# Talking-heads attention with a squared-ReLU feed-forward: queries loaded and turned in two parts, loads moved, four squares on VectorE, values products and transposes in front of score bursts

## The chip, the cores and the metric

One Trainium2 chip; the kernel runs on one of its cores. The metric is device time in microseconds (us) of one execution. The engines are named as in the profile: PE is TensorE (matmuls; PEld its weight loads), DVE VectorE, ACT ScalarE, POOL GpSimd, SP SyncE. PSUM has eight banks, which matmuls write and ACT and DVE read; SBUF is the working memory.

## What is computed

```
B, H, S, D = 8, 12, 448, 64
scores = (q @ k^T) / 8                               # per batch and head
scores = einsum('bhij,hg->bgij', scores, w_pre)      # heads mixed
attn   = softmax(scores over j)
attn   = einsum('bhij,hg->bgij', attn, w_post)       # heads mixed again
x      = (attn @ v), as [8*448, 768]
out    = (max(x @ w_in, 0) ** 2) @ w_out             # 768 -> 2048 -> 768
```

Inputs and output are f32 in HBM; on the chip operands are bf16 and sums f32.

## The kernel before

**Steps.** The attention of a batch is cut into 45 steps of up to ten queries (`IQ`), 360 steps in all. In a step the 120 rows of one tile are 10 queries x 12 heads, so that a matmul with a 120x120 matrix mixes the heads. `mix` (L456) does the first mix, one matmul into `m_ps` (L467), and the exponential on ACT (L471), with its sums; DVE takes the reciprocal `rc` (L478); POOL scales the second mixing matrix to `pn` (L481) and, for the last 64 keys, `en` (L484). `unmix` (L487) comes `LAG` = 4 steps later: three or four matmuls into `at_ps` (L496, L500) that mix and turn at once, and a copy to `at` on DVE (L502). Fifteen steps make a third of a batch, and `av_unit` (L246) then multiplies it with the values into `ot_ps` (L254, L261; two units a third) and copies it on ACT to `xt` (L267).

**Scores.** `score_burst` (L394) computes six heads of a block of up to 128 queries (L406; the last block of a batch packs its 64 queries in L412), each head into a PSUM bank, and ACT and DVE copy them to a tile `S`, of which there are two. `gather` (L423) copies ten queries' rows of all heads from `S` to a tile `G` by a DMA on SP's queue, ten steps (`AHEAD`) before the step that reads it; there are twelve `G`. `BURSTS` says at which gathered step of a block the two bursts of the next block are issued.

**Batch 0's first twenty steps** have no `S`: DVE multiplies the turned queries with the mixing weights (`mix_queries`, L218, into `w`, `tails` and `xt`), and `fused_part` (L445) takes six matmuls a step straight from keys and weighted queries into `m_ps` (L453). Steps 0 to 3 are weighted first (`NEAR`), then to 12 (`SOON`), then to 20 (`FUSED`).

**Queries, keys, values, weights.** POOL's queue loads them with a cast to bf16. Batch 0's queries and keys come in twelve loads, two of six heads a time, queries and keys in turn (L109 to L114); later batches in four loads (`load_qk`, `KQ_AT`, `KQ_LATER`: the steps), values in three (`load_v`, `V1_AT`, `V_LATER`), the FFN's weights in six and eight (`W1_AT`, `W2_AT`). Each query and key tile has one buffer, so a load waits until the batch before is turned. `turn_unit` (L227) does that: 28 transposes of 64x64 a unit and operand pair (L239) into two banks, and two copies (L241); six units a batch, at the steps of `TURN`.

**FFN.** `ffn1_unit` (L301): matmuls into `h_ps` (L308), ReLU on ACT to `hr` (L314), squares on POOL (L320; on DVE for the last third of batch 0). `ffn2_unit` (L347): eight matmuls a half (L353), the sum copied on DVE (L362) and stored.

**Order.** The order of PE and POOL is the program's own (`manual_schedule`); DVE, ACT and SP are ordered by a planner when the kernel is built, but for `issue_after`, which puts instructions behind a given one. Within a step: `mix`, then the units set for the step (`at_step`, `timed`: turns, value products), a share of the FFN's units (`fill`), `unmix`, up to two gathers with a burst where one is due, and another share. After a burst a second half of `ffn2_unit` is taken ahead, since it needs no new bank. A value product is set three steps after its third's last `unmix`; in the same step as the third third's product, the batch's FFN units join the list. `still` (L93) issues matmuls on zeros, whose result is not used, between the first transposes (`STILL`).

Of the kernel before, what the change touches and what calls it, by code (L numbers as in the profile page):

```python
# [14 lines left out]
B, H, S, D = 8, 12, 448, 64  # L15
DMODEL = H * D
DFF = 2048
NPAIR = H // 2
FT = DFF // 128
R = 4  # L20
RQ = 7
PQ = S // RQ
HQ = H // 2
IQ = 10
NT = 45
RG = H * IQ
FUSED = 20
# [5 lines left out]
BURSTS = {0: ([4, 8], [5, 8])}  # L33
for _b in range(1, B):
    STARTS[_b], FIRST[_b], BURSTS[_b] = (0, 128, 256, 384), (0, 13, 26, 39), ([5, 8], [5, 8], [6], [2, 4])
BURSTS[1] = ([5, 8], [7, 10], [6], [2, 4])
BURSTS[2] = ([7, 10], [5, 8], [6], [2, 4])
GATHERS_AT = 8
FIRST_AT = (3, 5, 7)
HALF = H // 2  # L40
TT = 15
TQ = TT * IQ
LAG = 4
AHEAD = 10
SCALE = 1.0 / 8.0
TURN = {0: (20, 22, 23, 24, 26, 27), 1: (24, 24, 24, 28, 28, 28), B: (2 + LAG,) * 3 + (17 + LAG,) * 3}
KQ_LATER = {1: (26, 28, 37, 41), B: (22, 25, 28, 31)}
V_LATER = {1: (30, 32, 34), B: (34, 37, 40)}
KQ_AT = {1: (4, 7, 10, 12), 2: (49, 51, 53, 55)}
W1_AT = (-1, 1, 3, 14, 16, 18)  # L50
W2_AT = (27, 29, 31, 33, 36, 39, 42, 45)
V1_AT = (46, 48, 24)
EARLY = ((21, 0, 0, 2), (29, 0, 2, 4), (38, 1, 0, 4), (52, 2, 0, 4))
FFN2_AT = 60
STILL = (10, 2, 2, 2, 1)
SOONEST = 3
MAIN = 3 * 128


@with_exitstack  # L60
def kernel(
# [36 lines left out]
    def stage_tile(name):  # L98
        return stage.tile([P, HQ, RQ, D], BF16, name=name, tag=name, bufs=1)

    def load(t, src, b, a, h0=0, h1=HQ):

        nc.gpsimd.dma_start(out=t[PQ * a:PQ * a + PQ, h0:h1, :, :].rearrange("p h r d -> p h (r d)"),
                            in_=src[b, HQ * a + h0:HQ * a + h1, :, :].rearrange("h (p r) d -> p h (r d)", r=RQ))

    staged = {}
    staged[0] = (stage_tile("qst"), stage_tile("kst"))
    ident = consts.tile([P, P], BF16, name="ident")
    for u in range(NPAIR // 2):  # L109
# [108 lines left out]
    def mix_queries(u, t0, t1):  # L218

        for y in range(2):  # L220
            qs = qTs[0][:, u + 3 * y, IQ * t0:IQ * t1].rearrange("p (t i) -> p t i", i=IQ)
            mixes[(u, t0)] = nc.vector.tensor_tensor(out=mixed(u, y, t0, t1).rearrange("p (t g i) -> p t g i", g=H, i=IQ),
                                    in0=qs.unsqueeze(2).to_broadcast([P, t1 - t0, H, IQ]),
                                    in1=wrep[:, u + 3 * y, :, :].unsqueeze(1).to_broadcast([P, t1 - t0, H, IQ]),
                                    op=ALU.mult)

    def turn_unit(b, which, u, eng=None):  # L227

        store, name = (qTs, "qT") if which == 0 else (kTs, "kT")
        if b not in store:  # L230
            store[b] = work.tile([P, NPAIR, S], BF16, name=name, tag=name, bufs=2)
        src = staged[b][which]
        got = [bank("tr_ps", BF16) for _ in range(2)]
        for r in range(RQ):
            c = PQ * (r if which == 0 or r == RQ - 1 else 2 * (r % 3) + r // 3)
            for hh in range(2):
                for x in range(2):
                    rs = slice(PQ * x, PQ * x + PQ)
                    nc.tensor.transpose(got[x][64 * hh:64 * hh + 64, c:c + PQ], src[rs, 2 * u + hh, r, :], ident[rs, rs])  # L239
# [61 lines left out]
    def ffn1_unit(b, ft, k=1, n0=0, n1=S):  # L301

        ps = bank("h_ps")
        n = n1 - n0
        for j in range(k):
            f = ft + j
            for c2 in range(NPAIR):
                nc.tensor.matmul(ps[:, n * j:n * j + n], lhsT=w1[f // 8][:, c2, f % 8 * 128:f % 8 * 128 + 128],  # L308
                                 rhs=xts[b][:, c2, n0:n1], start=(c2 == 0), stop=(c2 == NPAIR - 1))
        if n0 == 0 and ft % 2 == 0:  # L310
            h2ts[(b, ft // 2)] = ffnp.tile([P, 2, MAIN], BF16, name="h2", tag="h2", bufs=FT // 2 + 1)
        h2 = h2ts[(b, ft // 2)][:, ft % 2:ft % 2 + k, :]
# [211 lines left out]
    with tc.manual_schedule(engines={PE, POOL}):  # L524
# [19 lines left out]
        with tc.issue_after(mixes[(2, 0)].ins):  # L544
            mix_queries(1, NEAR, SOON)
            mix_queries(2, NEAR, SOON)
        loads = {}
        ahead = [FUSED]

# [26 lines left out]
        bounds = sorted({x[0] for x in EARLY} | {FFN2_AT, 2 * NT + 1 + LAG})  # L576
        end = len(steps) + LAG + 3
        for i in range(-1, end):
            for f in loads.get(i, []):
# [15 lines left out]
            rest = early[0] - i if early else (1 + LAG - i) % NT + 1  # L595
# [19 lines left out]
            if 2 < i < 6:  # L615
                with tc.issue_after(mixes[(2, NEAR)].ins):
                    mix_queries(i - 3, SOON, FUSED)
            if i in FIRST_AT:
                x = 2 * FIRST_AT.index(i)
                score_burst(0, 0, [x, x + 1])  # L620
            if i == 3:
                with tc.issue_after(mixes[(2, NEAR)].ins):
                    make_post()
                    make_orders()
                    clear_values()
            for _ in range(2 if i >= GATHERS_AT else 0):
                if ahead[0] > min(max(i + AHEAD, FIRST[0][1] - 1), len(steps) - 1):
                    break
                b2, t2 = steps[ahead[0]]
                gather((b2, t2))  # L630
                ahead[0] += 1
                blk2 = max(x for x in range(len(FIRST[b2])) if FIRST[b2][x] <= t2)
                nxt = blocks.index((b2, blk2)) + 1
                first = BURSTS[b2][blk2]
                if nxt < len(blocks) and t2 - FIRST[b2][blk2] in first:
                    x = first.index(t2 - FIRST[b2][blk2])
                    score_burst(*blocks[nxt], [3 * x, 3 * x + 1, 3 * x + 2])
                    if filler and filler[0][1] in second:
                        w, f = filler.pop(0)
                        f()  # L640
                        owed[0] -= w
            if i + 1 < end:
                fill(share)
        for j in sorted(timed):
# [34 lines left out]
```

## Time and profile before

| | us |
|---|---|
| Median of 3 runs | 583.04 (582.56 to 585.91) |
| The profiled execution | 583.95 |
| Its span in the profile | 582.2 |
| PE busy | 567.5 (97%) |
| DVE busy | 398.8 (69%) |
| ACT busy | 379.7 (65%) |
| POOL busy | 378.9 (65%) |
| First exponential of step 0 starts at | 16.43 |
| Step 0 of batch 1, 2, 3 and 4 (start of its exponential) | 73.6, 133.2, 201.3, 266.3 |

The span runs from the first to the last instruction; the execution's own time has 1.75 us around it. A line of a group gives the engine, the operation, names of what is written and read, the shape, the count, busy time and mean duration. In a timeline, the first number is the start, the second the time from there to the end of the group, and the bracket the idle time of the engine before it and what ended it. Matmuls overlap in the pipe, so a duration of 0.2 to 0.35 us is a latency; the distance between two starts is what a matmul costs.

### The profile page before, as it was taken

How to read it: one execution, taken by the hardware profiler on the slowest of the kernel's cores; microseconds unless marked ns; L12 is line 12 of the kernel's file. 1: busy time of each engine (PE TensorE's matmuls, PEld its weight loads, DVE VectorE, ACT ScalarE, POOL GpSimd, SP SyncE). 2: the span in 40 equal slices, each digit the busy share in tenths (PEclk: the TensorE clock that was granted, in tenths of full speed). 3: DMA queues.
4: the chain of work that ended last, by engine and by line, in shares of the span. 5: the costliest groups of instructions: out<-in, count | busy, mean ns of one | idle time of the engine just before them, and what ended most of it. 6: DMA issues, size and time to landing. Idle time of an engine off the chain costs nothing.

```text
span 582.2 us, 18463 instructions
## 1 busy us (share of the span) xinstructions
PE 567.5 (97%) x6750; PEld 362.6 (62%) x6752; DVE 398.8 (69%) x980; ACT 379.7 (65%) x1090; POOL 378.9 (65%) x844
## 2 busy tenths in 40 slices
PE   7999999999999999999999999999999999999996
PEld 3667777556566566566566665666665665666554
DVE  6858868778676777866877668867877668655011
ACT  2768978588876557864877648775777548862410
POOL 6657985655877448774778547785577647774830
PEclk9999999999999999999999999999999999999999
DMA  9999998797568864796558954697544865422113
GB/s 130 159 193 184 187 199 173 152 168 175 111 108 149 145 128 87 126 157 141 101 100 135 176 117 93 120 145 154 107 73 71 137 139 104 84 46 55 29 27 82
DMA packets 84043, 72.28 MB, mean 124 GB/s; under 512 B 18768, under 2 KB 80496, under 8 KB 83952
## 3 DMA queue, kind: packets, MB, share of 16 engines
q0 software_dynamic: 37856, 33.04, 37.1%
q1 hardware_dynamic: 45514, 37.86, 29.5%
q8 instruction: 53, 0.87, 0.6%
q10 hardware_dynamic: 582, 0.21, 0.2%
q14 instruction: 38, 0.31, 0.1%
HBM read 47.28 MB, written 11.01 MB: 100 GB/s over the span
## 4 chain that ended last, share of the span: by engine, by line
PE 89%; DMA 6%; ACT 2%; POOL 1%; issue 1%; DVE 1%; ACTq 0%; POOLq 0%
PE h_ps L308 24%; PE o_ps L353 24%; PE m_ps L467 11%; PE at_ps L496 10%; PE ot_ps L254 5%; DMA G<-S 5%; PE s_ps L406 5%; PE m_ps L453 4%; PE tr_ps L239 2%; PE ot_ps L261 2%; PE at_ps L500 2%; DMA kst<-in_k_dram 1%; PE s_ps L412 1%; ACT e L471 1%; ACT S L416 1%
## 5 line engine op out<-in xcount | busy, mean ns | idle before, releaser
L502 DVE CAST at<-at_ps 128x480 bf16<-128x480 f32 (+1 forms) x360 | 206.6, 592 | 63.1 <-PE at_ps L500 46.0
L471 ACT ACTIVATE e<-m_ps 120x448 bf16<-120x448 f32 x360 | 195.7, 550 | 82.1 <-PE m_ps L467 45.4
L481 POOL TENSOR_SCALAR pn<-post,rc 120x120 bf16<-120x120 bf16 (+1 forms) x340 | 122.4, 370 | 137.6 <-DVE rc L478 76.0
L308 PE MATMUL h_ps<-xt,w 128*128 128x448 bf16 (+2 forms) x960 | 165.8, 315 | 1.0 <-ACT S L416 0.9
L353 PE MATMUL o_ps<-w,h 128*128 128x384 bf16 x768 | 138.8, 326 | 0.1
L467 PE MATMUL m_ps<-G,pre 120*120 120x448 bf16 (+1 forms) x340 | 121.3, 357 | 2.5 <-ACT S L416 1.4
L308 PEld LDWEIGHTS <-w 128*128 128x128 bf16 x960 | 83.4, 98 | 54.1 <-issue 4.9
L496 PE MATMUL at_ps<-pn,e 120*128 120x120 bf16 x1080 | 115.8, 215 | 1.3 <-POOL pn L481 1.1
L496 PEld LDWEIGHTS <-e 120*128 120x128 bf16 x1080 | 85.9, 98 | 45.7 <-issue 3.6
L320 POOL TENSOR_TENSOR h<-hr 128x384 bf16<-128x384 f32 (+1 forms) x128 | 103.1, 806 | 11.1 <-ACT hr L314 9.5
L353 PEld LDWEIGHTS <-h 128*128 128x128 bf16 x768 | 72.4, 98 | 50.5 <-issue 8.0
L314 ACT ACTIVATE hr<-h_ps 128x448 f32<-128x448 f32 (+2 forms) x136 | 72.0, 530 | 47.0 <-PE h_ps L308 39.4
L416 ACT CAST S<-s_ps 128x448 bf16<-128x448 f32 x177 | 82.3, 551 | 11.1 <-PE s_ps L406 7.2
L418 DVE CAST S<-s_ps 128x448 bf16<-128x448 f32 x141 | 80.0, 615 | 3.9 <-DMA G<-S 2.8
L471 ACT ACTIVATION_READ_ACCUMULATOR e<-m_ps 120x1 f32 x360 | 75.5, 210 | 0.0
L362 DVE COPY osb<-o_ps 128x384 f32<-128x384 f32 x54 | 30.0, 556 | 55.4 <-PE o_ps L353 55.3
L478 DVE RECIPROCAL rc<-sm 120x1 f32<-120x1 f32 (+1 forms) x192 | 31.0, 162 | 40.6 <-ACT e L471 28.0
L467 PEld LDWEIGHTS <-pre 120*120 120x120 bf16 (+1 forms) x340 | 45.0, 132 | 17.5 <-issue 8.6
L267 ACT CAST xt<-ot_ps 128x450 bf16<-128x450 f32 (+1 forms) x48 | 25.7, 534 | 26.7 <-PE ot_ps L261 26.3
L484 POOL TENSOR_TENSOR en<-e,rc 120x128 bf16<-120x128 bf16 (+1 forms) x112 | 42.8, 382 | 0.0
L254 PE MATMUL ot_ps<-at,v 128*64 128x150 bf16 x864 | 41.7, 229 | 0.0
L406 PE MATMUL s_ps<-kT,qT 64*128 64x448 bf16 x276 | 39.0, 352 | 0.2
(66 smaller groups left out, 502.7 us busy)
## 6 DMA issues: line engine op xcount, KB each, us to landing
G<-S SPq DMA_DIRECT2D x276, 105.0 KB
out_dram<-osb POOLq DMA_DIRECT2D x48, 192.0 KB, 4.7
kst<-in_k_dram POOLq DMA_DIRECT2D x14, 336.0 KB, 5.9
qst<-in_q_dram POOLq DMA_DIRECT2D x14, 336.0 KB, 5.8
G<-S SPq DMA_DIRECT2D x70, 52.5 KB
v<-in_v_dram POOLq DMA_DIRECT2D x8, 384.0 KB, 9.1
w<-in_moe_w_in_dram POOLq DMA_DIRECT2D x6, 512.0 KB, 8.5
w<-in_moe_w_out_dram POOLq DMA_DIRECT2D x8, 384.0 KB, 9.2
```

The costliest lines, as they stand in the source:

```text
L254: nc.tensor.matmul(ps[64 * hh:64 * hh + 64, TQ * y:TQ * y + TQ], lhsT=vts[b % 2][:, g, r, :], rhs=at[:, r, g, :, :].rearrange("p t i -> p ...
L308: nc.tensor.matmul(ps[:, n * j:n * j + n], lhsT=w1[f // 8][:, c2, f % 8 * 128:f % 8 * 128 + 128], rhs=xts[b][:, c2, n0:n1], start=(c2 == 0 ...
L314: nc.scalar.activation(out=hr[:, 0:k * n], in_=ps[:, 0:k * n], func=ACT.Relu)
L320: eng.tensor_tensor(out=dst[:, :, x - o:y - o], in0=hr[:, :, x - n0:y - n0], in1=hr[:, :, x - n0:y - n0], op=ALU.mult)
L353: nc.tensor.matmul(ps[:, 0:384], lhsT=lhsT, rhs=w2[ft // 4][:, ft % 4, nt * 384:(nt + 1) * 384], start=(ft == 0), stop=(ft == FT - 1))
L416: nc.scalar.copy(out=sb[:, h, :], in_=ps[:, 0:S])
L418: nc.vector.tensor_copy(out=sb[:, h, :], in_=ps[:, 0:S])
L467: nc.tensor.matmul(ps[0:n, 0:S], lhsT=m[0:n, 0:n], rhs=Gs.pop(s)[0:n, :], start=True, stop=True)
L471: nc.scalar.activation(out=e[0:n, x, :], in_=ps[0:n, 0:S], func=ACT.Exp, scale=SCALE, accum_out=sm[0:n, x:x + 1])
L481: nc.gpsimd.tensor_scalar(out=esb[(b, t - z)][1][0:rows, :], in0=(post_gi if fused else post)[0:rows, :], scalar1=rc[0:rows, z:z + 1], sca ...
L496: nc.tensor.matmul(ps[:, RG * r:RG * r + RG], lhsT=e[0:n, tl % 2, P * r:P * r + P], rhs=pn[0:n, :], start=True, stop=True)
L502: nc.vector.tensor_copy(out=ats[(b, third)][:, 0:k, :, tl, :], in_=ps[:, 0:k * RG].rearrange("p (r g i) -> p r g i", r=k, i=IQ))
```

## The change

- *Queries in two parts.* Batch 0's queries are loaded as two of their seven row groups (`RF` = 2, 128 of 448 queries) for all heads first, in two loads with rows of 256 bytes in bf16; then the keys in six loads; then the other five row groups in two loads. The identity's memset is on DVE, and its mask comes after the fourth key load. `turn_unit` takes a range of row groups: the first part is turned at the start, the rest at step 3 (`REST_AT`). Weighted queries come in pieces of four steps, and one copy of the last keys is on DVE.
- The first score bursts of batch 0, the first gather and the last weighted queries come one step later.
- *Loads spread:* batch 2's queries and keys at steps 52, 54, 58, 61, batch 3's keys at 22 and 24 of batch 1, batch 2's values at 53, 55, 57 of batch 1, one load of batch 1's values at 49. The last two bursts in batch 1 come one step later.
- *Four squares:* of batch 0's second third, the squares of the FFN's upper half are on DVE.
- *Directly in front of bursts:* from batch 1 on, a third's value products are set in the step of the next burst that is three to seven steps away, directly in front of it (else as before); from batch 2 on, so are the transposes, at steps 8 (keys) and 22 (queries), which were at 6 and 21. Batch 0's transposes come in pairs, batch 1's first three at 20 instead of 24.
- `still`: 13, 3 and 3 matmuls instead of 10, 2, 2, 2 and 1.

```diff
@@ constants @@
+RF = 2
...
-BURSTS[1] = ([5, 8], [7, 10], [6], [2, 4])
+BURSTS[1] = ([5, 8], [7, 10], [6], [3, 5])
 BURSTS[2] = ([7, 10], [5, 8], [6], [2, 4])
-GATHERS_AT = 8
-FIRST_AT = (3, 5, 7)
+GATHERS_AT = 9
+FIRST_AT = (4, 6, 8)
+REST_AT = 3
...
-TURN = {0: (20, 22, 23, 24, 26, 27), 1: (24, 24, 24, 28, 28, 28), B: (2 + LAG,) * 3 + (17 + LAG,) * 3}
-KQ_LATER = {1: (26, 28, 37, 41), B: (22, 25, 28, 31)}
-V_LATER = {1: (30, 32, 34), B: (34, 37, 40)}
-KQ_AT = {1: (4, 7, 10, 12), 2: (49, 51, 53, 55)}
+TURN = {0: (21, 21, 24, 24, 27, 27), 1: (20, 20, 20, 28, 28, 28), B: (8,) * 3 + (22,) * 3}
+KQ_LATER = {1: (22, 24, 37, 41), B: (22, 25, 28, 31)}
+V_LATER = {1: (53, 55, 57), B: (34, 37, 40)}
+KQ_AT = {1: (4, 7, 10, 12), 2: (52, 54, 58, 61)}
...
-V1_AT = (46, 48, 24)
+V1_AT = (46, 49, 24)
...
-STILL = (10, 2, 2, 2, 1)
+STILL = (13, 3, 3)
+MERGE = 8
@@ first loads @@
-    def load(t, src, b, a, h0=0, h1=HQ):
-        nc.gpsimd.dma_start(out=t[PQ * a:PQ * a + PQ, h0:h1, :, :].rearrange("p h r d -> p h (r d)"),
-                            in_=src[b, HQ * a + h0:HQ * a + h1, :, :].rearrange("h (p r) d -> p h (r d)", r=RQ))
+    def load(t, src, b, a, h0=0, h1=HQ, r0=0, r1=RQ):
+        nc.gpsimd.dma_start(out=t[PQ * a:PQ * a + PQ, h0:h1, r0:r1, :].rearrange("p h r d -> p h (r d)"),
+                            in_=src[b, HQ * a + h0:HQ * a + h1, :, :].rearrange("h (p r) d -> p h (r d)", r=RQ)[:, :, r0 * D:r1 * D])
...
+    for x in range(2):
+        load(staged[0][0], q, 0, x, r1=RF)
+    nc.vector.memset(ident[:, :], 0.0)
     for u in range(NPAIR // 2):
-        for w, src in enumerate((q, k)):
-            for x in range(2):
-                load(staged[0][w], src, 0, x, 2 * u, 2 * u + 2)
-                if u + w == 0 and x == 1:
-                    masks.make_identity(nc, ident[:, :])
+        for x in range(2):
+            load(staged[0][1], k, 0, x, 2 * u, 2 * u + 2)
+        if u == 1:
+            masks.make_identity(nc, ident[:, :], nomemset=True)
+    for x in range(2):
+        load(staged[0][0], q, 0, x, r0=RF)
@@ turn_unit @@
-    def turn_unit(b, which, u, eng=None):
+    def turn_unit(b, which, u, engs=None, r0=0, r1=RQ):
...
-        for r in range(RQ):
+        for r in range(r0, r1):
...
-            (eng or nc.vector.tensor_copy)(out=store[b][:, u + 3 * x, :], in_=got[x][:, 0:S])
+            copy = engs[x] if engs else nc.vector.tensor_copy
+            copy(out=store[b][:, u + 3 * x, PQ * r0:PQ * r1], in_=got[x][:, PQ * r0:PQ * r1])
@@ ffn1_unit @@
-        eng = nc.vector if n0 >= 2 * TQ else nc.gpsimd
+        eng = nc.vector if n0 >= 2 * TQ or n0 and ft >= FT // 2 else nc.gpsimd
@@ order of the start @@
-    timed = {}
+    timed, front = {}, {}
+    burst_at = sorted(NT * b + FIRST[b][x] + y - AHEAD for b in range(1, B) for x in range(4) for y in BURSTS[b][x]
+                      if (b, x) != (B - 1, 3))
...
         for u in range(NPAIR // 2):
-            turn_unit(0, 0, u)
+            turn_unit(0, 0, u, r1=RF)
             mix_queries(u, 0, NEAR)
-            if u == 1:
-                with tc.issue_after(mixes[(1, 0)].ins):
-                    mix_queries(0, NEAR, SOON)
+        still(STILL[1])
+        for u in range(NPAIR // 2):
             if u == 2:
+                with tc.issue_after(mixes[(2, 0)].ins):
+                    mix_queries(0, NEAR, 2 * NEAR)
+
+            def between(out, in_):
+                with tc.issue_after(mixes[(0, NEAR)].ins):
+                    mixes["kT"] = nc.vector.tensor_copy(out=out, in_=in_)
+
+            turn_unit(0, 1, u, (nc.scalar.copy, nc.scalar.copy if u < 2 else between))
+            if u == 0:
+                still(STILL[2])
+            else:
                 for t in range(SOONEST):
-                    fused_part(t, 0)
-            else:
-                still(STILL[1 + 2 * u])
-            turn_unit(0, 1, u, nc.scalar.copy)
-            if u < 2:
-                still(STILL[2 + 2 * u])
-        for t in range(SOONEST):
-            fused_part(t, 1)
...
+        for t0 in range(NEAR, SOON, NEAR):
+            with tc.issue_after(mixes["kT" if t0 == NEAR else (2, t0 - NEAR)].ins):
+                for u in range(t0 == NEAR, NPAIR // 2):
+                    mix_queries(u, t0, t0 + NEAR)
@@ order of the steps @@
                         for x, u in enumerate(turn_units(b + 1)):
-                            at_step(i + TURN.get(b, TURN[B])[x], u)
+                            if b in TURN:
+                                at_step(i + TURN[b][x], u)
+                            else:
+                                front.setdefault(i + TURN[B][x], []).append(u)
...
                 if t1 % TT == TT - 1:
+                    j = min([x for x in burst_at if 3 <= x - i < 8 and b1] + [i + MERGE])
                     for u in av_units(b1, t1 // TT):
-                        at_step(i + 3, u)
-                if t1 == NT - 1:
-                    at_step(i + 3 if b1 else FFN2_AT, (0, lambda b1=b1: filler.extend(ffn_units(b1))))
...
+                        if j in burst_at and b1:
+                            front.setdefault(j, []).append(u)
+                        else:
+                            at_step(i + 3, u)
+                    if t1 == NT - 1:
+                        more = (0, lambda b1=b1: filler.extend(ffn_units(b1)))
+                        if not b1:
+                            at_step(FFN2_AT, more)
+                        elif j in burst_at:
+                            front.setdefault(j, []).append(more)
+                        else:
+                            at_step(i + 3, more)
+            if i == REST_AT:
+                for u in range(NPAIR // 2):
+                    turn_unit(0, 0, u, r0=RF)
...
                     x = first.index(t2 - FIRST[b2][blk2])
+                    for w, f in front.pop(i, []):
+                        f()
+                        owed[0] -= w if not FFN2_AT <= i < 2 * NT else 0
                     score_burst(*blocks[nxt], [3 * x, 3 * x + 1, 3 * x + 2])
```

The bounds by which the FFN's units are spread over a batch's steps end two steps later (`3 + LAG` for `1 + LAG`), as the units start two steps later.

More of the change, by code (lines that the diff above doesn't have):

```diff
@@ L528 @@
         for u in range(NPAIR // 2):
-            turn_unit(0, 0, u)
+            turn_unit(0, 0, u, r1=RF)
             mix_queries(u, 0, NEAR)
-            if u == 1:
-                with tc.issue_after(mixes[(1, 0)].ins):
-                    mix_queries(0, NEAR, SOON)
+        still(STILL[1])
+        for u in range(NPAIR // 2):
             if u == 2:
-                for t in range(SOONEST):
-                    fused_part(t, 0)
-            else:
-                still(STILL[1 + 2 * u])
-            turn_unit(0, 1, u, nc.scalar.copy)
-            if u < 2:
-                still(STILL[2 + 2 * u])
-        for t in range(SOONEST):
-            fused_part(t, 1)
-        with tc.issue_after(mixes[(2, 0)].ins):
-            mix_queries(1, NEAR, SOON)
-            mix_queries(2, NEAR, SOON)
+                with tc.issue_after(mixes[(2, 0)].ins):
[7 more added lines that the diff above has]
+            else:
+                for t in range(SOONEST):
+                    fused_part(t, u - 1)
+        for t0 in range(NEAR, SOON, NEAR):
+            with tc.issue_after(mixes["kT" if t0 == NEAR else (2, t0 - NEAR)].ins):
+                for u in range(t0 == NEAR, NPAIR // 2):
+                    mix_queries(u, t0, t0 + NEAR)
         loads = {}
@@ L575 @@
             at_step(x, (0, lambda third=third, q0=q0, q1=q1: begin(ffn1_third(third, q0, q1))))
-        bounds = sorted({x[0] for x in EARLY} | {FFN2_AT, 2 * NT + 1 + LAG})
+        bounds = sorted({x[0] for x in EARLY} | {FFN2_AT, 2 * NT + 3 + LAG})
         end = len(steps) + LAG + 3
@@ L592 @@
                         for x, u in enumerate(turn_units(b + 1)):
-                            at_step(i + TURN.get(b, TURN[B])[x], u)
+                            if b in TURN:
+                                at_step(i + TURN[b][x], u)
+                            else:
+                                front.setdefault(i + TURN[B][x], []).append(u)
             early = [x for x in bounds if x > i]
-            rest = early[0] - i if early else (1 + LAG - i) % NT + 1
+            rest = early[0] - i if early else (3 + LAG - i) % NT + 1
             rest = min(rest, end - i) if i > len(steps) - NT // 2 else rest
@@ L610 @@
                 if t1 % TT == TT - 1:
+                    j = min([x for x in burst_at if 3 <= x - i < 8 and b1] + [i + MERGE])
                     for u in av_units(b1, t1 // TT):
-                        at_step(i + 3, u)
-                if t1 == NT - 1:
-                    at_step(i + 3 if b1 else FFN2_AT, (0, lambda b1=b1: filler.extend(ffn_units(b1))))
-            if 2 < i < 6:
-                with tc.issue_after(mixes[(2, NEAR)].ins):
-                    mix_queries(i - 3, SOON, FUSED)
+                        if j in burst_at and b1:
[13 more added lines that the diff above has]
+                    turn_unit(0, 0, u, r0=RF)
+            if FIRST_AT[0] <= i < FIRST_AT[0] + 3:
+                with tc.issue_after(mixes[(2, SOON - NEAR)].ins):
+                    mix_queries(i - FIRST_AT[0], SOON, FUSED)
             if i in FIRST_AT:
@@ L621 @@
             if i == 3:
-                with tc.issue_after(mixes[(2, NEAR)].ins):
+                with tc.issue_after(mixes[(2, SOON - NEAR)].ins):
                     make_post()
@@ L641 @@
                         owed[0] -= w
+            for w, f in front.pop(i, []):
+                f()
+                owed[0] -= w
             if i + 1 < end:
```

## The prediction

> **What bounds the kernel now.** I read the page's busy table, then stretches of the span, the waits of the one bad stretch, and timelines where work of the change stands.
>
> ```profile
> PE 567.5 (97%) x6750; PEld 362.6 (62%) x6752; DVE 398.8 (69%) x980; ACT 379.7 (65%) x1090; POOL 378.9 (65%) x844
> ```
>
> TensorE is the bound: the others have a third of the span free. A gain must come from TensorE's idle time or from its lost time between matmuls. The busy time by stretches says where it idles (columns: stretch, its length, then busy time and instructions of PE, PEld, DVE, ACT, POOL; clock, DMA share, GB/s):
>
> ```profile
> 60.00:100.00 40.00, 37.57 (x529) 29.36 (x526) 31.02 (x83) 34.23 (x107) 31.81 (x69) 1.00 1.04 190
> 100.00:140.00 40.00, 37.63 (x625) 24.53 (x624) 30.31 (x76) 28.60 (x86) 23.38 (x59) 1.00 0.85 165
> ...
> 200.00:300.00 100.00, 99.80 (x1311) 63.37 (x1310) 75.31 (x185) 68.98 (x200) 68.98 (x156) 1.00 0.63 118
> ```
>
> From 60 to 140 us, the end of batch 0 and all of batch 1, TensorE idles 2.43 + 2.37 = 4.8 us; from 200 to 300 only 0.2. The waits from 55 to 150 us (total, times, longest) name what it waited for:
>
> ```profile
> ACT S L416 <- DMA G<-S: 3.1, 2, 2.6
> ...
> PE m_ps L467 <- ACT S L416: 1.4, 1, 1.4
> ...
> PE at_ps L496 <- POOL pn L481: 1.1, 1, 1.1
> ```
>
> The 1.4 is a wait for score copies that still hold the PSUM banks, and they waited themselves until gathers had read the old S; the 1.1 is a late `pn` on POOL. A third, 0.87 before `h_ps` at 88.57, is again a wait for score copies. At the start, the chain runs through the last key load:
>
> ```profile
> 14.33 0.41 PE L239 MATMUL tr_ps<-ident,kst 64*64 64x64 bf16 x27 [0.61 <-DMA kst<-in_k_dram]
> ...
> 14.67 3.62 PE L453 MATMUL m_ps<-kT,w 128*120 128x448 bf16 x18
> ...
> 16.43 0.54 ACT L471 ACTIVATE e<-m_ps 120x448 bf16<-120x448 f32 x1 [0.68 <-PE m_ps L453]
> ```
>
> From 14.67 on TensorE never waits long, so what lets it begin earlier is worth its full time. Last, what a change of the matmuls' form costs in the steady state:
>
> ```profile
> 318.85 0.35 PE L467 MATMUL m_ps<-G,pre 120*120 120x448 bf16 x1
> 319.04 0.32 PE L496 MATMUL at_ps<-pn,e 120*128 120x120 bf16 x3
> 319.20 0.35 PE L467 MATMUL m_ps<-G,pre 120*120 120x448 bf16 x1
> 319.48 0.39 PE L254 MATMUL ot_ps<-at,v 128*64 128x150 bf16 x6
> ...
> 320.76 0.25 PE L261 MATMUL ot_ps<-at,v 128*64 128x80 bf16 x4
> 320.84 0.38 PE L254 MATMUL ot_ps<-at,v 128*64 128x150 bf16 x6
> 321.03 0.25 PE L261 MATMUL ot_ps<-at,v 128*64 128x80 bf16 x4
> 321.22 0.33 PE L496 MATMUL at_ps<-pn,e 120*128 120x120 bf16 x3
> ```
>
> After `m_ps`, `at_ps` starts 0.19 us later but `ot_ps` 0.28: going to the half-width form costs 0.09. After the last `ot_ps` group the next start is 0.19 us away instead of 0.08: leaving costs 0.11.
>
> **The start: loads.** Before, twelve loads of 112 KB; issues on POOL about 0.59 us apart; the last key load is issued at 8.41 and lands at 14.29 (the trace's DMA records); the five before it land 4.6 us after their issue (4.14 and less for the first ones), the last 5.9. After, two query loads of 384 runs each (0.69 us on POOL, as the later whole loads of 384 runs at 27.04 and 31.82; the first 0.2 more), then six key loads at 0.60 and the mask step of 0.35 between (its memset goes to VectorE): the last key load is issued at 1.28 + 0.89 + 0.69 + 4 x 0.60 + 0.35 + 0.60 = 6.2. By 4.6 it lands at 10.8, 3.5 us earlier; by 5.9 at 12.1, 2.2 earlier. By packets: 896-byte packets took 88 ns, 384-byte 51, 128-byte 32, so 256-byte ones some 41 (an estimate on that line), and 896-byte packets passed at 216 per us, 19 in flight. Query part 768 x 41 / 19000 = 1.7 us, keys 768 / 216 = 3.6, against 1536 / 216 = 7.1 before: 1.8 us earlier. Ends 1.8 and 3.5; I take 3.2, since the 4.6 held for five loads out of six.
> The first packet rows show no break, only a slope. The Trainium skill's "DMA: Bandwidth & Descriptors" (Specifications) says that below 512 bytes a DMA does a read-modify-write and loses line rate; the query part writes 256 bytes per run. By the slope it is 1.7 us; if that rule doubled it (the page has no factor; an estimate), the start would gain 1.7 us less and the sum come to 577.0. No row here has 256 bytes.
>
> **The start: work moved.** The other five sevenths of the queries are turned at step 3, no longer under a load wait but in TensorE's full stream: 60 of 84 transposes; 84 take 0.93 us at 296.39, so 0.66, plus 0.09 and 0.11 for the forms: 0.86. Their loads are the next two in POOL's queue (v and w1 one place later, not needed before step 21). They are wanted at about 14.5 and land at 13.8 to 15; I take no wait, at most 1.0. VectorE's mixes up to step 12 total the same, in more pieces; it has all first queries at 7 instead of 11.85 us, which covers six more issues and one key copy (0.35). If this cover is gone the exponentials wait 1 us. Extra still matmuls (19 for 17) lie under the load wait. Net 3.2 - 0.9 = 2.3; ends 1.8 - 0.9 - 1.0 = -0.1 and 2.8.
>
> **Stalls of 60 to 140 us.** Before the stall at 78.80, POOL did squares at 76.27 and 77.72 (0.70 each) and a value load (0.80, at 76.90) ahead of the `pn`. The two squares go to VectorE: `pn` 1.4 us earlier, and the 1.09 is gone; I take 1.0. The squares, 300 wide, cost VectorE 0.46 us each by its rows of 128 and 168 elements (0.28 and 0.33), up to 0.9 when it runs beside POOL's (0.50 and 0.77 at 84.7); VectorE is 78% busy there, and they may wait on ACT's `hr` (0.55 the longest). Queued behind them are `at` copies and `rc`, so `pn`; each has four steps in hand, about 6 us. Price without that cover 4 x 0.55 = 2.2.
> At 117.52, score copies waited 2.64 us for gathers and TensorE lost 1.42, so 1.2 were covered. Batch 1's last bursts come one step later (about 1.5 us), leaving 1.1, which is covered; the value and key loads around it move to other steps (their issues stay 0.7 to 0.8 each on POOL). I take 1.3. At 88.57 (0.87) and the small ones (0.30, 0.33): the next batch's loads are spread from steps 49-55 to 52-61, so the gathers have fewer packets beside them; 0.7 together. SP issues the gathers in order; after batch 1's last burst its first gather from that S comes one step later, with ten steps in hand. Sum 3.0; ends 4.8 (all gone) and -1 (they move and VectorE's squares bring one).
>
> **Merged visits.** Values products with transposes, directly before a burst, save one visit to the narrow forms: 0.09 + 0.11 less a direct change of form. That change's price: from the last transpose to the first value product 0.12 us at ten places, so 0.10 net. By the burst steps, 18 merges: 2 in batch 1, 3 in each of 2 to 6, 1 in 7: 1.8 us. Ends 0 and 3.6. Batch 0's six turns are in three pairs: 3 x 0.2 = 0.6. Together 2.4. Nothing else is removed: matmuls, copies and exponentials are the same. The moved units' copies move with them (ACT 2 x 0.53, VectorE 6 x 0.31), and FFN units start and end two steps later.
>
> **Sum.** 2.3 + 3.0 + 2.4 = 7.7 us. The profiled execution took 583.95 (span 582.2 and 1.75 around it), 0.91 above the median of 583.04: it would become 576.25, the median 575.3.
>
> **Rivals.**
> *Banks run out in front of the bursts* (the slower side). At steps 8 and 22 of batches 2 to 6 fourteen banks' worth is written in a row, with eight to be had. TensorE needs 0.93 + 1.7 + 0.8 = 3.4 us for it; VectorE six copies in 1.87 and three of 0.616, 3.7, and its `at` copies. If each of the ten places loses what 117.52 lost (1.42, the next bank) and what the burst at 164.54 lost (0.58, its own banks), that is 20.0, and the median 595.3. It decides from 0.77 us a place (7.7 / 10); over 1% slower from 1.35. Against it: at 296.39 transposes and value products end at 299.06 and the 12-matmul burst at 299.72 starts 0.25 us after the matmul before it; nearly the same pile, no wait.
> *The start gains nothing*: VectorE or the second query part is late. 583.04 - 5.4 = 577.6.
> *The stalls move*: S has two buffers before and after, and the gathers must read the old one. 583.04 - 4.7 = 578.3.
> *All ends good*: 2.8 + 4.8 + 4.2 = 11.8, so 571.2.
> *TensorE's clock falls while it waits for keys.* The first 512-column matmuls here came 0.43 us apart, the 18 of 448 columns at 14.67 0.20. At the early pace (0.376 for 448) the 24 of steps 0 to 3 cost 4.2 more: 579.5. Against it: the waits before were as long (0.96), the rows give a granted clock of 1.00 throughout, and the faster pace held. The Trainium skill's "TensorE: Matmul & The Clock Gate" (What's actually happening) has half rate after an idle window of about 3.4 us; the trace's first matmuls agree, and none of the new waits should be that long.
>
> **How the numbers follow.** Forecast 0.56, with its own range 571.5 to 578.5; all good 0.10; start lost 0.07; stalls move 0.08; clock 0.03; banks 0.16. About 1% (5.8 us, 577.2 and 588.9) is what a measurement can tell. Faster by over 1%: all good, 0.10, and of the forecast 0.46, together 0.56. Within 1%: the forecast's other 0.10, the start lost, the stalls and the clock, together 0.28. Slower by over 1%: banks, 0.16. Range 567 to 586: it holds every case but most of the banks' (586 is 1.1 a place), and below 567 lies only more than all good.
>
> **What would show it.** Right: the first `e` at 13 to 13.5 us instead of 16.43; 60 transposes in the stream behind step 3 without a DMA wait; TensorE busy over 38.5 of 40 us in the two stretches; no `pn` wait near 77; `ot_ps` with the next start an `s_ps`. Wrong: `s_ps` or `tr_ps` waiting for `S` or `qT` copies in batches 2 to 6; VectorE's `w` as the last releaser of `m_ps`; a slow first 12 us.

## The result, and the profile after

| | before | after |
|---|---|---|
| median, us (18 runs each) | 583.08 (581.25 to 586.71) | 585.92 (583.86 to 588.35) |
| ratio after / before | | 1.0051 [1.0032, 1.0069] |
| the profiled execution, us | 583.95 | 583.95 |
| its span, us | 582.2 | 581.6 |
| first exponential of step 0 starts at, us | 16.43 | 12.8 |

The change costs half a per cent, where 1.3% less was forecast. The profiled execution of the changed kernel lies 2 us under its median, so its trace shows less than the whole loss; two more traces of it are used below. Part of the loss lies outside the span: the changed kernel's runs have 2.25 to 2.36 us around it, where before's have 1.8 on average.

The busy table of the changed kernel, and the same stretches as in the prediction with one more (length, then busy time and instructions of PE, PEld, DVE, ACT, POOL; clock, DMA share, GB/s):

```profile
PE 568.2 (98%) x6753; PEld 363.9 (63%) x6754; DVE 405.0 (70%) x998; ACT 377.6 (65%) x1089; POOL 376.9 (65%) x837
```

```profile
60.00:100.00 40.00, 38.96 (x645) 30.56 (x642) 34.30 (x92) 34.08 (x105) 29.17 (x64) 1.00 1.04 196
100.00:140.00 40.00, 38.40 (x557) 24.61 (x558) 32.36 (x81) 30.89 (x95) 23.55 (x59) 1.00 0.73 152
200.00:300.00 100.00, 99.44 (x1300) 62.90 (x1298) 76.05 (x188) 69.54 (x202) 67.11 (x150) 1.00 0.65 119
300.00:400.00 100.00, 98.72 (x1084) 61.30 (x1083) 76.36 (x171) 67.03 (x194) 68.82 (x155) 1.00 0.73 131
```

The two bad stretches got better, as forecast: TensorE idles 1.04 + 1.60 us instead of 4.8. The steady state got worse: 0.56 us idle from 200 to 300 instead of 0.20, and 1.28 instead of 0.17 in the next hundred. What TensorE waits for is new as well (total, times, longest):

```profile
PE s_ps L420 <- issue: 1.6, 1, 1.6
PE s_ps L414 <- ACT e L479: 1.4, 8, 0.2
...
PE s_ps L414 <- DVE at L510: 0.8, 2, 0.4
```

The first row is a single wait in the packed burst of batch 2; "issue" means that the profile shows nothing that it waited for, so its cause stays open. In the other rows score matmuls wait until ScalarE's exponential has read an `m_ps`, or VectorE's copy an `at_ps`: for a free bank. Before has one such wait, of 0.6 us.

The rows hold only the last piece of each wait; matmuls that start late one after another count as busy in the pipe. To see it all I took the starts of all matmuls between 20 and 540 us and subtracted what each needs when it streams. Inside the score bursts 9.7 us are lost that way, against 2.7 in before's trace; in two more traces of after 9.9 and 9.2, and 2.1 in a second one of before. Some 1.9 of the 9.7 are the unexplained wait in batch 2 (0.9 and 1.4 in the two other traces); the rest is the loss that the experiments below follow up. Where it falls is seen at step 8 of batch 4, in TensorE's timeline of the changed kernel (start, time to the group's end, ...):

```profile
271.92 1.05 PE L246 MATMUL tr_ps<-ident,kst 64*64 64x64 bf16 x84
272.90 0.39 PE L262 MATMUL ot_ps<-at,v 128*64 128x150 bf16 x6
...
274.64 1.07 PE L414 MATMUL s_ps<-kT,qT 64*128 64x448 bf16 x6
...
276.88 1.16 PE L414 MATMUL s_ps<-kT,qT 64*128 64x448 bf16 x5
...
278.22 0.35 PE L414 MATMUL s_ps<-kT,qT 64*128 64x448 bf16 x1 [0.18 <-ACT e L479]
...
278.50 1.31 PE L316 MATMUL h_ps<-xt,w 128*128 128x448 bf16 x6
```

Transposes, value products and the first burst stand together as the change wants it, and that burst takes 1.00 us to the next start. The *next* burst follows 2.24 us after it, and its six matmuls take 1.62 us, 276.88 to 278.50. From 271.9 to 278.50 no FFN matmul is issued. In before's trace, at the same step, FFN matmuls (`h_ps`) stand between the two bursts, which are 4.47 us apart, and the second takes 0.69 us (282.89 to 283.58):

```profile
278.42 0.85 PE L406 MATMUL s_ps<-kT,qT 64*128 64x448 bf16 x6
...
279.77 1.30 PE L308 MATMUL h_ps<-xt,w 128*128 128x448 bf16 x6
...
281.30 1.30 PE L308 MATMUL h_ps<-xt,w 128*128 128x448 bf16 x6
...
282.89 0.74 PE L406 MATMUL s_ps<-kT,qT 64*128 64x448 bf16 x6
283.58 0.38 PE L467 MATMUL m_ps<-G,pre 120*120 120x448 bf16 x1
```

The busy times of VectorE (the third) and ScalarE (the fourth) in the changed kernel say why the banks are not back:

```profile
271.90:278.50 6.60, 6.42 (x172) 4.15 (x170) 6.46 (x19) 4.89 (x15) 2.21 (x5) 1.00 0.50 109
274.70:278.50 3.80, 3.62 (x28) 1.56 (x26) 3.80 (x11) 3.75 (x12) 0.45 (x2) 1.00 0.53 127
```

From 274.7 on both engines that empty the banks are busy almost without a break, 3.80 and 3.75 of 3.80 us. VectorE copies the six turned keys, half of twelve score banks and every `at`; ScalarE copies the value products and the other half of the score banks, and has the exponentials behind them. The releases in the trace show both: the second burst's matmuls start after a score copy and an `at` copy on VectorE and after three exponentials on ScalarE, and the last two, 0.30 and 0.53 us after the one before, after exponentials. So it is not VectorE alone.

The burst after step 8's loses in each of batches 2 to 6: 0.94 in batch 2 and 1.05 in the others (0.11 to 0.40 before, where the two are 3.4 to 4.5 us apart). The merged burst of step 8 itself loses 0.25 in batch 2 and 0.44 in the others (0.22 before). Other bursts lose in some batches only: 0.88 and 0.85 at step 31 of batches 4 and 5, and 1.30 at step 43 of batch 5 (393.59).

Why no FFN matmuls? The FFN is spread over the steps by an account. Every unit set in front of a burst is charged to it, `owed[0] -= w`: three turn units of 250 and two value products of 800, so 2350 at once, which stops the FFN's units for about three steps. Before, the same 2350 were charged at step 6, where these transposes and products stood together (from 274.75 in its trace), two steps ahead of the burst of step 8, so that FFN units came again before the burst after it.

### The profile page after: what moved, and what is told of

It reads as the page before. It is cut to its first block, busy times and chain, and to the rows that moved or that the text cites. A ratio compares the mean times of both kernels' runs of the same rounds, so it can differ in the third digit from the quotient of the medians.

```text
span 581.6 us, 18472 instructions
## 1 busy us (share of the span) xinstructions
PE 568.2 (98%) x6753; PEld 363.9 (63%) x6754; DVE 405.0 (70%) x998; ACT 377.6 (65%) x1089; POOL 376.9 (65%) x837
## 4 chain that ended last, share of the span: by engine, by line
PE 85%; DMA 5%; ACT 5%; DVE 2%; POOL 1%; issue 1%; SPq 0%; ACTq 0%; POOLq 0%
PE o_ps L361 25%; PE h_ps L316 24%; PE m_ps L475 11%; PE at_ps L504 9%; PE ot_ps L262 5%; PE s_ps L414 4%; DMA G<-S 4%; ACT e L479 3%; PE m_ps L461 2%; PE tr_ps L246 2%; PE ot_ps L269 2%; PE at_ps L508 2%; ACT S L424 1%; PE s_ps L420 1%; DMA kst<-in_k_dram 1%
## 5 line engine op out<-in xcount | busy, mean ns | idle before, releaser
L504 PEld LDWEIGHTS <-e 120*128 120x128 bf16 x1080 | 88.3, 98 | 46.1 <-ACT S L424 2.0
L328 POOL TENSOR_TENSOR h<-hr 128x384 bf16<-128x384 f32 (+1 forms) x124 | 100.4, 811 | 15.8 <-ACT hr L322 14.4
L479 ACT ACTIVATION_READ_ACCUMULATOR e<-m_ps 120x1 f32 x360 | 77.1, 214 | 0.0
L414 PE MATMUL s_ps<-kT,qT 64*128 64x448 bf16 x276 | 43.2, 352 | 2.9 <-ACT e L479 1.4
```

Source lines behind the costliest of these rows:

```text
L479: nc.scalar.activation(out=e[0:n, x, :], in_=ps[0:n, 0:S], func=ACT.Exp, scale=SCALE, accum_out=sm[0:n, x:x + 1])
L504: nc.tensor.matmul(ps[:, RG * r:RG * r + RG], lhsT=e[0:n, tl % 2, P * r:P * r + P], rhs=pn[0:n, :], start=True, stop=True)
```

## The experiments

Thirteen kernels, and three more traces of the two that are compared. "Before" is measured with each group: 583.07, 582.66, 582.91 and 582.58. Two theories stood against each other: the merged visits starve the banks; or the start's lead and the spread loads are what is lost.

**no_front**: all of the change but the visits in front of bursts.

```
-TURN[B] = (8,) * 3 + (22,) * 3
+TURN[B] = (2 + LAG,) * 3 + (17 + LAG,) * 3
 (units by at_step, products three steps after their third, bounds 1 + LAG as before)
```

> The changed kernel with the units in front of the bursts put back: transposes of batches 2 to 6 at steps 6 and 21, value products three steps after their third, the filler's bounds as before; start, loads, squares, turns of batches 0 and 1 as changed. Theory (the units in front cost it): in the changed kernel's trace the lead over before falls from 7.1 us at the first step of batch 3 to 1.8 at the last of batch 7, and the second burst of each of batches 2 to 6 loses 0.94 to 1.06 us instead of 0.1 to 0.4. Without them the lead stays: 576 to 578, ratio 0.988 to 0.992. Rival (the start, or the clock in it, costs what two traces do not show; the medians stand 3.4 us further apart than the spans): 580 to 583, with a granted clock under 0.999 in half of the runs.

Measured 579.21 (578.80 to 580.39), ratio 0.9941 [0.9918, 0.9965]. It lies between the two expectations: the visits account for the loss, but not all of the forecast comes back without them.

**front_only**: the visits in front of bursts put into the kernel before, nothing else (`MERGE`, `burst_at`, `front`, `TURN[B]`, bounds `3 + LAG`).

> The kernel before with only the units in front of bursts (and the filler's bounds with them). Theory: slower by 3.5 to 5.5 us, ratio 1.006 to 1.010, with 0.9 us and more lost in the second burst of batches 2 to 6. Rival (start and clock): faster by 1 to 2 us, as 18 merges at 0.1 us would give, ratio 0.997.

Measured 588.93 (588.50 to 589.83), ratio 1.0108 [1.0082, 1.0135]; 8.0 us are lost in bursts. So the visits alone cost 5.9 us, and 6.7 on top of the rest. Its trace also has half the clock from 8.4 to 15.2 us, but that is not where the time goes: from step 0 of batch 2 to the end it takes 454.5 us, the three traces of the changed kernel 454.7 to 457.1, and before's two 449.0 and 448.7, no_front's 448.9. This settles which part it is.

**no_debt**: the changed kernel, but what stands in front of a burst is not charged.

```
 for w, f in front.pop(i, []):
     f()
-    owed[0] -= w if not FFN2_AT <= i < 2 * NT else 0
 score_burst(...)
```

> The changed kernel, but a unit in front of a burst is not charged to the filler's account, so FFN units come between the merged burst and the next one. Theory, cause within it: the second burst follows too soon (2.2 us after the first instead of 3.5 to 4.5), since the account is in debt and no FFN unit comes between; then its loss falls to 0.1 to 0.4 and the time by 3 to 5 us to 581 to 583 (ratio 0.996 to 1.000). Rival cause (fourteen banks in a row before the merged burst itself): within 1 us of the changed kernel, 585 to 586.

Measured 579.07 (577.07 to 583.24), ratio 0.9941 [0.9918, 0.9964]. One line gives back 6.85 us, all that the visits cost and more than expected. The merges and the later bounds are all there; FFN units now go between the two bursts, as TensorE's timeline of this kernel at the same place shows:

```profile
279.32 1.06 PE L414 MATMUL s_ps<-kT,qT 64*128 64x448 bf16 x6
280.31 0.40 PE L475 MATMUL m_ps<-G,pre 120*120 120x448 bf16 x1
280.55 1.30 PE L316 MATMUL h_ps<-xt,w 128*128 128x448 bf16 x6
...
282.25 1.30 PE L316 MATMUL h_ps<-xt,w 128*128 128x448 bf16 x6
...
283.83 0.74 PE L414 MATMUL s_ps<-kT,qT 64*128 64x448 bf16 x6
284.52 0.38 PE L475 MATMUL m_ps<-G,pre 120*120 120x448 bf16 x1
```

The bursts are 4.51 us apart, and the second takes 0.69 us (283.83 to 284.52) instead of 1.62. Inside bursts 2.5 us are lost in the whole trace.

**burst_later**: the charge stays, the second burst of a block comes two steps later.

```
+for _b in range(2, B):
+    BURSTS[_b] = (BURSTS[_b][0], [5, 10], [6], [2, 4])
```

> The changed kernel, charges as changed, but the second burst of step 11 in batches 2 to 7 two gathered steps later (13). Theory (the second burst comes too soon after the merged one): it then finds its banks free, loss 0.1 to 0.4 instead of 1.05; the other late places (steps 30 and 43) stay, so 2.5 to 4 us off the changed kernel's 585.9: 582 to 583.5. If the account's debt hurts by itself, wherever the burst is: 585 to 586.

Measured 582.16 (580.63 to 586.98), ratio 1.001 [0.9985, 1.0035]. The moved bursts lose 0.1 to 0.47 instead of 1.05, those at steps 31 and 43 keep 0.85 to 1.30, and 5.5 us remain in bursts. So 3.8 of the 6.7 us come back with the charge in place, by moving the second burst away. In its trace the two bursts of batch 4 are 5.26 us apart (275.60 and 280.86), and two groups of FFN matmuls stand between them here too (277.74 and 279.47): the time between the bursts and the FFN matmuls that fill it are not told apart by these runs.

**both**: no_debt and burst_later together.

> The changed kernel with its units in front of bursts uncharged and the second burst of step 11 two gathered steps later. Both cures have the same aim (FFN matmuls between merged burst and next burst), so theory has them not add: 578 to 579.5. If they cure different losses: 575 to 577.

Measured 577.65 (576.35 to 580.89), ratio 0.9907 [0.9874, 0.9940]: the best version, 5.3 us under before and 8.3 under the changed kernel. Bursts lose 1.6 us. It lies between the two expectations, 1.4 us under no_debt alone. TensorE's steady state is full:

```profile
200.00:300.00 100.00, 99.98 (x1315) 63.68 (x1313) 75.79 (x187) 70.24 (x203) 69.86 (x156) 1.00 0.63 119
300.00:400.00 100.00, 99.98 (x1116) 63.21 (x1114) 75.81 (x178) 67.89 (x199) 69.62 (x158) 1.00 0.74 136
```

**front_late**: merged only at steps 22 and 40, the third third's products meant to stay where they were (`t1 < NT - 1` added to the condition, with `i + MERGE` left as the fallback).

> The changed kernel with units in front of the bursts only at steps 22 and 40; what was put in front at step 8 is back at step 6. Theory: step 22 has no burst close behind, step 40 has one three steps on; the five losses of 1.05 at the second burst go, 12 merges stay: 579 to 581. If merging itself costs: half of the way between 579.2 and 585.9, about 583.

Measured 590.65 (589.23 to 591.30), ratio 1.0142 [1.0111, 1.0173]: a miss. The edit did something else. For the third third, `i + 8` is step 11, itself a burst step, so these products and the FFN's new units still went in front of a burst, while the bounds were set two steps sooner: the FFN's list ran empty from step 6 to 11. The burst at step 8 loses 1.02 in each of batches 2 to 6, and `pn` waits of 1.1 appear (218.59 and 357.28). No FFN matmuls around the bursts, and it is worse than the change: against my number, for the mechanism.

**front_late2**: the same with the third third's products truly at `i + 3` (`END`, a step that never comes, in place of `i + MERGE`).

> What the run with units in front at steps 22 and 40 alone meant to be; there the third third's products fell in front of step 11 by the changed kernel's own rule, and the FFN's list began there, after five steps without FFN matmuls. Here those products and the FFN's list come three steps after their third. Theory: no merged burst has another close behind with the account in debt, except 40 and 43: 578.5 to 581. If merging at 22 and 40 costs too: 583 or more.

Measured 580.70 (578.37 to 582.36), ratio 0.995 [0.9925, 0.9974]; 2.4 us in bursts. It lies 1.5 above no_front, and the intervals overlap: with the charge in place, merging at 22 and 40 shows no gain.

**loads_only** and **no_squares** split what no_front keeps. The first is before with the moved loads, batch 1's later bursts, batch 0's paired turns and the squares; the second is no_front with the four squares back on POOL.

```
-eng = nc.vector if n0 >= 2 * TQ or n0 and ft >= FT // 2 else nc.gpsimd
+eng = nc.vector if n0 >= 2 * TQ else nc.gpsimd
```

> The kernel before with only the moved loads, the four squares, batch 1's later last bursts and batch 0's and 1's turns. By the difference of the medians with and without them in the first group (581.33 and 579.21): 2 us faster, 581.0, ratio 0.996. By the prediction's 3.0 + 0.6: 579.5.

> The kernel without the units in front of bursts (start and loads as changed), and the four squares back on POOL. If the squares are what frees pn near 77 us: a PE wait of about 1 us for pn comes back there and the time is 0.5 to 1.5 us above 579.2. If the loads do it: within 0.5 us of 579.2.

loads_only: 579.42 (577.99 to 581.12), 0.9944 [0.9921, 0.9968]. My guess from the group before it, 2 us, was too low: it is 3.2. no_squares: 579.21 (577.22 to 584.76), 0.9941 [0.9913, 0.9970]. In its trace the `pn` wait of before is back (1.15 at 80.96; 0.67 in no_front, at 76.01), and the time is that of no_front: the squares are worth nothing that can be measured.

**start_only**: before with the new start alone.

> The kernel before with only the changed start: queries in two parts, pieces of weighted queries, first bursts a step later, still matmuls. Theory: its first exponential at 12.8 us, its lead 2.6 us after step 5 and to the end: 580.4, ratio 0.9955. Rival (the clock falls in the new start): the trace's lead may be the same, but half of the runs show a clock under 0.999 and the median is 583 or more.

Measured 581.33 (578.57 to 584.95), 0.9974 [0.9950, 0.9998]: 1.7 us, where 2.6 was expected.

**both_old_start**: both, with the loads, turns and `still` of before's start.

> The best version (units in front uncharged, second burst later, moved loads and squares) with the start of the kernel before. Theory (the new start is worth 1.2 to 1.6 us from step 5 on, part of it lost in batch 1's waits): 578.0 to 579.2, against 577.65. Rival (the lead is lost wholly): 577.3 to 577.9.

Measured 579.20 (578.28 to 581.27), 0.9938 [0.9910, 0.9967]: the new start is worth 1.5 us here.

**light_start** and **light_old_start**: is the start's lead given back because the DMA engines are full from 60 to 100 us (share 1.04)? Both leave out half of the loads of `w_out` and fill these weights with a constant; neither has the visits in front of bursts, and one has the new start, one the old.

```
+if x % 2:
+    nc.gpsimd.memset(w2[x // 2][:, c:c + 2, :], 0.01)
+    return
```

> The kernel without units in front of bursts (579.2), with half of the w_out loads (every second one, 1.5 of 3 MB in bf16, steps 29 to 45) left out and a memset on POOL in its place, so the output is not the reference's. Read against the next one. Theory (the start's lead of 2.6 us is given back as waits for gathers, since the DMA engines are full up to 95 us and the bytes do not come sooner): with fewer bytes the lead stays, and this one is 1.5 to 2.5 us faster than the next. Rival (the lead is lost in TensorE's or VectorE's own order): the two are within 0.7 us, as with all loads (579.2 against 579.4).

> The kernel before with the moved loads, squares and turns (579.4), and the same half of the w_out loads left out, output not the reference's. Theory: 0 to 1 us faster than 579.4, as its gathers already wait little; 1.5 to 2.5 us slower than the one with the new start. Rival: the same time as that.

Measured 578.55 (578.17 to 579.38) and 579.11 (578.83 to 581.28): 0.56 apart, with a DMA share from 60 to 100 us of 0.89 and 0.87. The lead did not come back with less to load, so the theory of the full DMA engines is not borne out.

**after_look1**, **after_look2**, **before_look**: two further traces of the changed kernel and one of before.

> The changed kernel once more, one profiled look. If a usual execution loses more in the bursts themselves: losses in bursts above 10 us in its trace (9.7 in the first look). If elsewhere: bursts lose the same 9.7, and 2 us more stand in waits of batches 0 to 2 (gathers, pn, score copies) or in a stretch of half clock.

> The same kernel, a third look. As for the look before it; both together say which places vary from execution to execution and which do not: theory has the second burst's 1.05 us constant and the waits of batches 0 to 2 vary.

> The kernel before, a second look. Its first look had its first exponential at 16.43 us, one microsecond later than the two runs with the same start (15.4 and 15.6). Theory: here it is at 15.4 to 15.7, so the new start's lead at step 5 is 1.2 to 1.6 us and not 2.6.

Single times 586.38, 588.86 and 581.90. The loss in bursts is nearly the same in all three traces of after (9.7, 9.9, 9.2) and in both of before (2.7, 2.1), and so does not come from one profile. before_look has its first exponential at 15.5, so that before's first trace had begun a us late; and the end of batch 0 differs from run to run (last section). Elsewhere the three traces of the changed kernel differ too: in the later two the merged burst at step 8 of batch 5 itself waits, for 1.44 and 1.09 us, put down to a score copy (348.5 and 351.4); the first has no such wait.

## Why the prediction was wrong, point by point

*The step that failed* is the costing of the merged visits: "Nothing else is removed: matmuls, copies and exponentials are the same", with the moved units priced by their copies alone, and "FFN units start and end two steps later" put at nothing. The saving itself came out to the tenth. Over all entries into and exits from the narrow forms (64*128, 128*64 and 64*64 in the rows) the changed kernel has 22.2 us against 24.0 in no_front: 1.8 for 18 merges. What was not costed is the account that the moved units are charged to. With it the visits cost 6.7 us net by medians, where a saving of 1.8 was forecast; no_debt shows that the charge is what does it. By traces it is 7.4 more in bursts less 1.8, so 5.6. Of the difference between the two views 0.4 us lie outside the span (2.3 around it, against 1.83 to 1.90 in no_front); the rest is not settled. The prediction carried before's 1.75 around the span over to the changed kernel: no_debt (2.15), both (2.18) and burst_later (2.31) have the longer time too, front_only (1.75), start_only (1.81) and loads_only (1.80) do not, and its cause stays open.

*The rival "Banks run out"* (0.16) named the right resource and the wrong place. It asked whether the merged burst waits, at ten places, and found at one of them in before's trace, a pile of step 22, that it does not. At step 22 that holds in batches 3 to 6; at step 8 nearly: 0.44 for 0.22. The loss is in the burst *after* step 8's, and in some later ones. The loss per place from which the prediction let this rival decide, 0.77, was near the real size by chance: the burst after step 8's loses 0.65 to 0.95 more than before, at five places. The wrong sign that the prediction named is what the waits show in part: `s_ps` waits for banks in batches 2 to 6, though mostly for the readers of `m_ps` and `at_ps` and not for `S` or `qT` copies.

*Stalls of 60 to 140 us:* 3.0, and 0.6 for batch 0's pairs. loads_only has both and gains 3.2: right in size. The two stretches have 38.96 and 38.40 us busy where over 38.5 was forecast for each; in after_look2's trace the first has 34.71, with the wait of the last section. But of the 3.0, 1.0 was ascribed to the squares, and no_squares has the same time without them; a `pn` wait of 0.67 remained, where none was forecast.

*The start:* 2.3. The last key load lands at 10.32 instead of 14.29, 4.0 earlier and not 3.2. But the prediction worked from a trace in which this load was late: in four others with the old start it landed at 12.8 to 13.3, 4.3 to 4.9 us after its issue and not 5.9, so that the new start's lead is 2.5 to 3.0. (The first loads, which the prediction puts at "4.14 and less", took 4.1 to 4.6.) The first exponential comes at 12.8, and at 12.8 to 13.8 in all traces with the new start, where 13 to 13.5 was forecast; with the old start and the full clock it comes at 15.4 to 15.8. The five sevenths are turned without a DMA wait:

```profile
10.70 0.41 PE L246 MATMUL tr_ps<-ident,kst 64*64 64x64 bf16 x28
11.04 3.62 PE L461 MATMUL m_ps<-kT,w 128*120 128x448 bf16 x18
14.59 0.73 PE L246 MATMUL tr_ps<-ident,qst 64*64 64x64 bf16 x60
15.25 1.35 PE L461 MATMUL m_ps<-kT,w 128*120 128x448 bf16 x6
```

They take 0.66 (14.59 to 15.25), as priced, with their loads landed at 12.06 and 13.85. By step 5 the lead, between traces that differ in the start, is 1.0 to 1.7, and in the medians the start is worth 1.7, 1.5, 0.6 and 0.2 (start_only; both; the light pair; no_front against loads_only). The term was too large, by 0.6 to 2.1; which of these values is the true one stays open, since the kernels' runs spread over 2 to 6 us.

*TensorE's clock while it waits for keys* (0.03): not in after's traces. In two traces with the old start the clock was half: in front_only's from 8.4 to 15.2, with the first exponential at 17.7, and in loads_only's from 8.4 to 11.8, with no delay (15.62).

## What to carry to other kernels

When work is moved, look up everything that counts it: here a schedule's account paid for it at the new place and withheld the very work that kept the next burst away. A pile of bank writers is judged by the burst that comes after it, not by the one that it stands in front of, and by how much the engines that empty the banks still have to do. And a gain that fails should be tried with its side effect taken out: one line turned the change from 2.8 us slower to 4.0 faster.

## What was unexpected of the hardware

**A wait of some 2.5 to 4.5 us can cost the clock as well.** At batch 0's end score copies wait for gathers, in some executions briefly, in others for several us. The timeline of after_look2, then its stretches (the clock is the third number from the end):

```profile
69.52 1.84 ACT L424 CAST S<-s_ps 128x448 bf16<-128x448 f32 x4 [4.59 <-DMA G<-S]
...
70.11 0.48 PE L504 MATMUL at_ps<-pn,e 120*128 120x120 bf16 x3 [4.48 <-ACT S L424]
```

```profile
65.60:70.10 4.50, 0.03 (x1) 0.00 (x0) 0.50 (x1) 0.58 (x2) 2.07 (x4) 0.96 1.12 214
69.80:73.20 3.40, 3.09 (x23) 2.65 (x24) 1.70 (x4) 3.04 (x9) 0.00 (x0) 0.50 0.93 185
73.20:80.00 6.80, 6.80 (x91) 5.58 (x89) 5.75 (x16) 6.08 (x19) 4.62 (x10) 1.00 0.62 142
```

TensorE stands still for 4.48 us; the clock is half from 69.8 to 73.2, and the 3.09 busy us in it cost some 1.5 us more (an estimate: half of them). With a wait of 2.73 us (no_debt, up to 69.70) the clock was half for 6.83 us from 68.9 on, with one of 2.49 (no_squares, up to 68.90) for 3.41 from 69.7 on, with one of 2.3 (before_look) not at all. The Trainium skill's "TensorE: Matmul & The Clock Gate" (What's actually happening) gives half rate after an idle window of 3413 ns that runs freely. The lengths agree, 3.41 and twice 3.41; the idle time that sufficed was shorter than the page's window. At the start the clock fell without any such wait: in front_only and loads_only from 8.4 us on, behind a stretch (5.0 to 8.4) in which TensorE was busy for 2.08 and 2.09 of 3.40 us and no single wait was over 0.82. In before's trace, busy for 2.29 us there, it did not fall. The prediction had excluded this rule for waits that short. How much of the spread of the kernels' times comes from this was not worked out.

**Rows of 256 bytes showed no penalty.** The query part's loads, 96 KB in such rows, landed at 5.23 and 6.15 us; before's first loads, 112 KB in rows of 896 bytes, at 5.51 and 6.71. Its 768 packets of 256 bytes took 41 ns in the median, the value that the prediction had read off between its rows for other sizes. The read-modify-write below 512 bytes of the Trainium skill's "DMA: Bandwidth & Descriptors" (Specifications) cost nothing that the start shows.

**Changing from one narrow form to another costs as much as entering one**: 0.10 to 0.115 us from value products to score matmuls, against 0.09 for entering and 0.11 for leaving.
